# Forty-two elementwise instructions of a gated MLP layer moved from GpSimd to the Vector engine

## The chip, the cores and the metric

The kernel runs on one core of one Trainium2 chip. The metric is the time of one execution on the device in microseconds (us); of several runs the median counts. The engines are called as the profile calls them: PE (TensorE, with PEld for its weight loads), DVE (the Vector engine), ACT (the Scalar engine), POOL (GpSimd) and SP (the engine that issues most of the DMAs).

## What is computed

Three layers follow one another on B = 2 batches of S = 768 tokens.

```python
def _attn_ref(q, k, v, alpha):          # 8 heads of 48
    for t in range(S):
        state = alpha[:, :, t, :, None] * state + np.einsum('bhd,bhe->bhde', k[:, :, t], v[:, :, t])
        y[:, :, t] = np.einsum('bhd,bhde->bhe', q[:, :, t], state)
...
def _moe_ref(x, w_in, g_ln, w_sg, b_sg, w_out):   # d_model 384, d_ff 1024
    h = gelu(x @ w_in)
    u, v = h[..., :512], h[..., 512:]
    v_n = (v - mean(v)) / sqrt(var(v) + 1e-6) * g_ln
    v_s = np.einsum('ts,bsd->btd', w_sg, v_n) + b_sg[None, :, None]
    return x + (u * v_s) @ w_out
...
def _moe2_ref(x, w_gate, w_local, w1, w2):        # 8 experts
    # each token has one expert e: the argmax of its logits, or the expert of the token before it
    out[b, s] = p[e] * (np.maximum(x[b, s] @ w1[e], 0.0) @ w2[e])
```

The second layer is the one the change touches: x is the attention output, `u * v_s` is "the gate's product".

## The kernel before

**Split numbers.** Most products of the second and third layer are made from pairs. `split` (lines 160 to 162) takes a tile `src`: ACT writes its rounded high part (line 161), and an engine that the caller names writes the low part, `src` minus the high part (line 162). `mm3` (line 373) then issues three matmuls for each product: high by high, high by low, low by high.

**The engine is a table's choice.** `pick(way)` (line 157) returns DVE where the lowest bit of `way` is set, otherwise POOL. Three tables use it: `XS_E` for the low part of the attention output in `x_split` (12 pieces of 128x384: two batches, three row groups, two halves of the tokens); `NS_E` for the low part of the normalised v in `norm` (12 pieces of 128x512); and `SG` for the gate in `gmlp_s` (16 pieces), bit 0 for the product, bit 1 for the low part of that product.

**The gate, step by step** (`gmlp_s`, from line 478). For a batch b, a part hf of the tokens and one of four row groups d: PE adds up 18 matmuls in `pvs`; DVE scales it and adds the bias (line 493, tile `vs`); the engine of bit 0 multiplies by u (line 495); ACT writes the high part of the product into `g` (line 161) and the engine of bit 1 the low part (line 162). `gmlp_out` (line 499) multiplies the four `g` by `wo` on PE (`po`), DVE adds the result to x (line 511), and `route` (line 514) computes logits, keeps and expert slots: matmuls `pr` on PE, then a chain of short DVE instructions to `kf`, a matmul `pkr`, a DVE scan `er`, a matmul `pe`. Batch 0 has parts of 384 and 384 tokens, batch 1 of 512 and 256 (`SPL`).

```python
        eng = [self.pick(way), self.pick(way >> 1)]
...
        nc.vector.scalar_tensor_tensor(out=vs, in0=pv, scalar=self.gln[:, d:d + 1], in1=self.bsg[:, sl],
                                       op0=ALU.mult, op1=ALU.add)
        eng[0].tensor_tensor(out=vs, in0=vs, in1=us[d][:, sl], op=ALU.mult)
        self.split(hi, lo, vs, eng[1])
```

**What else runs beside the gate of batch 0.** The four pieces of `w_out` are prepared there (`w64_split`): on DVE four instructions each, in lines 318, 320, 321 and 324 (tile `w_wo`, 128x384), on ACT two, and on POOL the low part `wo_lo`. Then `x_split` of batch 1 (tile `xhl`).

**What sets the order.** A scheduler orders each engine's instructions ahead of time by its own estimate of when operands are there; an engine then runs its list strictly in that order, and an instruction whose operand is late holds up all behind it. A different engine for an instruction therefore also changes the order on other engines.

The stages in time of the profiled execution: attention with the first projections to about 145 us, then the gate and routing of batch 0, its counterpart of batch 1 from about 216 to 260, the experts from 274 to the end.

Of the kernel before, what the change touches and what calls it, by code (L numbers as in the profile page):

```python
# [60 lines left out]
XS = 16  # L61
SPL = (384, 512)
SELM = 0
SG = (0, 0, 2, 3, 0, 0, 0, 3, 2, 0, 0, 3, 0, 2, 0, 1)
XS_E = (0, 2, 0, 0, 0, 0, 1, 0, 0, 0, 0, 0)
NS_E = (0, 0, 0, 2, 1, 0, 2, 0, 0, 1, 3, 0)
XEE = 0
NUNIT = 21

# [3 lines left out]
class Layer:  # L73
# [329 lines left out]
    def x_split(self, b, xT):  # L403
        nc = self.nc
        xhl = []
        for k in range(KM):
            t = self.unit([P, 2, S], F32R, f"xhl_{b}_{k}")
            for hf in range(2):
                sl = slice(hf * HALF, (hf + 1) * HALF)
                self.split(t[:, 0, sl], t[:, 1, sl], xT[k][:, sl], self.pick(XS_E[b * 6 + k * 2 + hf]))  # L410
            xhl.append((t[:, 0], t[:, 1]))
        return xhl

    def gmlp_h(self, b, xhl, vhl, us, seq):
# [35 lines left out]
        def norm(j):  # L450
# [6 lines left out]
            for i in range(G):  # L457
                v2 = v2s[i]
                nc.scalar.activation(out=v2, in_=v2, func=AF.Identity, scale=vr[:, 1, i:i + 1], bias=vr[:, 0, i:i + 1])
                self.split(vh[:, i, :], vl[:, i, :], v2, self.pick(NS_E[b * 6 + len(vhl)]))  # L460
                vhl.append((vh[:, i, :], vl[:, i, :]))
# [16 lines left out]
    def gmlp_s(self, b, hf, d, vhl, us):  # L478
# [10 lines left out]
        hi, lo = self.gt[:, d % m, 0], self.gt[:, d % m, 1]  # L489
        way = SG[(2 * b + hf) * 4 + d]  # L490
        eng = [self.pick(way), self.pick(way >> 1)]
# [535 lines left out]
```

## Time and profile before

| | us |
|---|---|
| median of 3 runs (lowest, highest) | 429.46 (428.47, 433.92) |
| the profiled execution's own time | 431.54 |
| its span, first to last instruction | 429.8 |
| PE busy | 403.0 |
| DVE busy | 299.3 |
| POOL busy | 142.1 |
| mean granted TensorE clock | 0.889 of full speed |

[...] A row of the timeline gives start, duration, engine, line, operation, output and inputs, the shape, how many instructions were merged, and in brackets how long the engine had been idle before it and whom it waited for. A duration on DVE includes some 0.05 to 0.1 us in which the next instruction already runs, so rows of merged instructions are shorter than the sum.

### The profile page before, as it was taken

The page shows a single profiled execution, that of the slowest core. Times are in us where ns is not written, and L with a number is a line of the kernel's source. Part 1 is how long each engine was busy: PE and PEld are TensorE (multiplying, and loading weights), DVE is VectorE, ACT ScalarE, POOL GpSimd, SP SyncE. Part 2 cuts the span into 40 slices and gives each one's busy share as a digit, 9 for nine tenths or more (in the row PEclk, how much of TensorE's full clock was granted, in tenths as well). Part 3 has the DMA queues.
Part 4 walks back from the last instruction along what each step waited for, and adds up shares of the span by engine and source line. Part 5 has one row for each costly group of instructions (what it writes and reads, how often), then busy time and mean ns, then how long its engine had stood idle before and what let it go on. Part 6 is the DMA issues. An engine that isn't in the chain of part 4 may idle for free. (4 is left out here: it accounts for less than half of the span.)

```text
span 429.8 us, 7588 instructions
## 1 busy us (share of the span) xinstructions
PE 403.0 (94%) x2751; PEld 347.8 (81%) x2751; DVE 299.3 (70%) x694; ACT 202.1 (47%) x465; POOL 142.1 (33%) x156
## 2 busy tenths in 40 slices
PE   5899999999999996999999988999998999999992
PEld 2776666778886986798888885799888999999991
DVE  7969694954847698677866867673798866894220
ACT  2343443564787533426572432542793655763110
POOL 2315332754037457700304423375131110101101
PEclk9555555589999998999999998899998999999998
DMA  8993558220204220101060254958988457100000
GB/s 222 281 217 95 174 155 245 88 68 15 88 2 139 66 73 0 57 1 58 0 221 2 73 160 140 329 150 240 374 289 297 143 198 278 53 2 29 30 2 24
DMA packets 34742, 54.54 MB, mean 127 GB/s; under 512 B 6243, under 2 KB 24957, under 8 KB 34704
## 3 DMA queue, kind: packets, MB, share of 16 engines
q1 hardware_dynamic: 32528, 48.08, 35.7%
q0 software_dynamic: 2176, 5.98, 4.7%
q8 instruction: 22, 0.36, 0.4%
q14 instruction: 16, 0.13, 0.1%
HBM read 46.91 MB, written 5.55 MB: 122 GB/s over the span
## 5 line engine op out<-in xcount | busy, mean ns | idle before, releaser
L377 PE MATMUL pmy_e<-we_e_hi,hhl_e 128*128 128x384 f32 x256 | 68.5, 343 | 2.4 <-DVE hhl_e L756 1.8
L377 PE MATMUL ph_e<-xhl_e,we_e_hi 128*128 128x256 f32 x384 | 70.4, 284 | 0.1
L162 DVE TENSOR_TENSOR we_e_lo<-wr_e,we_e_hi 128x384 fp32r<-128x384 f32 (+1 forms) x112 | 61.5, 604 | 10.8 <-ACT we_e_hi L161 5.5
L161 ACT ACTIVATE we_e_hi<-wr_e 128x384 fp32r<-128x384 f32 (+1 forms) x112 | 54.6, 568 | 24.6 <-PE pmy_e L377 12.9
L377 PEld LDWEIGHTS ph_e<-xhl_e,we_e_hi 128*128 128x128 f32 x384 | 60.4, 191 | 0.6 <-DVE xhl_e L162 0.6
L770 POOL DMA_INDIRECT out_dram<-my_e,sid x16 | 20.5, 1280 | 105.8 <-DVE my_e L769 76.3
L377 PE MATMUL ph_e<-xhl_e,we_e_lo 128*128 128x256 f32 x192 | 54.1, 283 | 0.0
L377 PEld LDWEIGHTS pmy_e<-we_e_hi,hhl_e 128*128 128x128 f32 x256 | 47.2, 191 | 3.3 <-DVE hhl_e L756 2.0
L231 POOL TENSOR_SCALAR_AFFINE_SELECT at<-at 128x384 f32<-128x384 f32 x32 | 25.6, 820 | 64.9 <-ACT at L229 64.9
L377 PE MATMUL pmy_e<-we_e_lo,hhl_e 128*128 128x384 f32 x128 | 43.3, 339 | 0.1
L755 ACT ACTIVATE hhl_e<-ph_e 128x256 fp32r<-128x256 f32 x64 | 22.9, 385 | 40.9 <-PE ph_e L377 40.7
L377 PEld LDWEIGHTS ph_e<-xhl_e,we_e_lo 128*128 128x128 f32 x192 | 36.8, 192 | 0.0
L756 DVE SCALAR_TENSOR_TENSOR hhl_e<-ph_e,hhl_e 128x256 fp32r<-128x256 f32 x64 | 24.7, 416 | 15.0 <-ACT hhl_e L755 14.9
L377 PE MATMUL pvs<-sg_hi,v_hi 128*128 128x384 f32 (+2 forms) x96 | 32.9, 343 | 0.0
L377 PE MATMUL pvs<-sg_lo,v_hi 128*128 128x384 f32 (+2 forms) x96 | 32.1, 335 | 0.0
L377 PE MATMUL pvs<-sg_hi,v_lo 128*128 128x384 f32 (+2 forms) x96 | 31.1, 336 | 0.0
L279 PE MATMUL py<-at,io 128*64 128x128 f32 (+1 forms) x192 | 30.1, 383 | 0.0
L377 PE MATMUL po<-g,wo_hi 128*128 128x384 f32 (+2 forms) x96 | 26.3, 354 | 3.9 <-ACT g L161 3.2
L227 PE MATMUL sc<-io 48*128 48x128 f32 x192 | 29.1, 406 | 0.0
L262 ACT ACTIVATE state<-pds,bc 112x48 f32<-112x48 f32 x40 | 12.1, 301 | 34.8 <-PE pds L260 25.6
L227 PEld LDWEIGHTS sc<-io 48*128 48x128 f32 x192 | 22.5, 278 | 6.6 <-issue 3.7
L769 DVE TENSOR_SCALAR my_e<-pmy_e,xs_e 128x384 f32<-128x384 f32 x16 | 9.8, 611 | 21.9 <-PE pmy_e L377 21.7
(200 smaller groups left out, 876.0 us busy)
## 6 DMA issues: line engine op xcount, KB each, us to landing
wr_e<-in_moe_w_dram SPq DMA_DIRECT2D x32, 768.0 KB, 7.4
io<-in_alpha_dram SPq DMA_DIRECT2D x16, 169.8 KB, 5.0
io<-in_k_dram SPq DMA_DIRECT2D x16, 168.0 KB, 4.9
io<-in_q_dram SPq DMA_DIRECT2D x16, 168.0 KB, 5.0
io<-in_v_dram SPq DMA_DIRECT2D x16, 144.0 KB, 4.9
sraw<-in_moe_w_sg_dram SPq DMA_DIRECT2D x3, 768.0 KB, 4.5
x2d<-xt SPq DMA_DIRECT2D x12, 192.0 KB, 2.0
x<-y SPq DMA_DIRECT2D x24, 72.0 KB, 2.2
```

The source lines that it names most:

```text
L161: return (self.nc.scalar.activation(out=hi, in_=src, func=AF.Copy), eng.tensor_tensor(out=lo, in0=src, in1=hi.bitcast(F32), op=ALU.subtract))
L162: eng.tensor_tensor(out=lo, in0=src, in1=hi.bitcast(F32), op=ALU.subtract))
L227: nc.tensor.matmul(sc[j][:, cs], kf[r, cs], qf[r, cs], start=True, stop=True)
L231: nc.gpsimd.affine_select(out=at[:, j], in_=at[:, j], compare_op=ALU.is_ge, fill=0.0, base=0, pattern=[[0, NCH], [1, P]], channel_multipli ...
L262: nc.scalar.activation(out=state[:, s0 + c + 1, :], in_=pds[:112, cd], func=AF.Identity, scale=bc[:, c:c + 1])
L279: nc.tensor.matmul(py[64 * j:64 * j + m, cs], g["v"][:, o:o + m], at[:, j, c, :], start=True, stop=not inter)
L377: self.nc.tensor.matmul(out, l[a], r[c], start=start and i == 0 and p == 0, stop=stop and i == n - 1 and p == 2)
L755: nc.scalar.activation(out=hh, in_=ph, func=AF.Relu)
L756: nc.vector.scalar_tensor_tensor(out=hl, in0=ph, scalar=0.0, in1=hh.bitcast(F32), op0=ALU.max, op1=ALU.subtract)
L769: nc.vector.tensor_scalar(out=y, in0=py, scalar1=prob[i], scalar2=None, op0=ALU.mult)
L770: nc.gpsimd.indirect_dma_start(out=self.out2, out_offset=bass.IndirectOffsetOnAxis(ap=sid[:, i:i + 1], axis=0), in_=y, in_offset=None, bou ...
```

## The change

Three tables change, no other line. The gate's 16 products and 16 low parts, the 12 low parts of the attention output and the 12 of the normalised v all go to DVE. The pieces that leave POOL are 12 products, 10 low parts of the gate, 11 of the attention output and 9 of v: 42.

```diff
-SG = (0, 0, 2, 3, 0, 0, 0, 3, 2, 0, 0, 3, 0, 2, 0, 1)
-XS_E = (0, 2, 0, 0, 0, 0, 1, 0, 0, 0, 0, 0)
-NS_E = (0, 0, 0, 2, 1, 0, 2, 0, 0, 1, 3, 0)
+SG = (3,) * 16
+XS_E = (1,) * 12
+NS_E = (1,) * 12
```

On DVE, at about 77 to 90 us, where the attention's last two decays are prepared (`aw`, `io`) and the last pieces of `w_in` (`w_wu`), the low parts `xhl` of batch 0 now stand between them:

```order
 L200 COPY begins<-io_1_2_656 112x3
+L162 TENSOR_TENSOR xhl_0_790<-x_91,xhl_0_790 128x384
 L320 SCALAR_TENSOR_TENSOR w_wu_652<-w_wu_652 128x512
 L201 SCALAR_TENSOR_TENSOR aw_1_2_1027<-io_1_2_656,begins 112x384
+L162 TENSOR_TENSOR xhl_0_790<-x_91,xhl_0_790 128x384
+L162 TENSOR_TENSOR xhl_1_795<-x_92,xhl_1_795 128x384
 L321 SCALAR_TENSOR_TENSOR w_wu_652<-w_wu_652 128x512
+L162 TENSOR_TENSOR xhl_2_800<-x_93,xhl_2_800 128x384
 L202 COPY bc_1_2_1028<-aw_1_2_1027 112x3
 L207 TENSOR_TENSOR io_1_2_656<-io_1_2_656,aw_1_2_1027 112x384
```

The two remaining `xhl` pieces follow behind the next L203 and L204, ahead of the last decay.

On DVE in the gate of batch 0, first part, with the last piece of `w_out` (`w_wo_1563`); the scaling of pieces 2 and 3 (L493) now stands ahead of two of that weight's instructions, and both products and low parts follow:

```order
 L318 TENSOR_SCALAR w_wo_1563<-w_wo_1563 128x384
+L493 SCALAR_TENSOR_TENSOR vs_2_0_1645<-pvs_2_0_1625,gln,bsg 128x384
+L493 SCALAR_TENSOR_TENSOR vs_3_0_1669<-pvs_3_0_1650,gln,bsg 128x384
 L320 SCALAR_TENSOR_TENSOR w_wo_1563<-w_wo_1563 128x384
+L495 TENSOR_TENSOR vs_2_0_1645<-vs_2_0_1645,u_2_1275 128x384
+L495 TENSOR_TENSOR vs_3_0_1669<-vs_3_0_1669,u_2_1275 128x384
 L321 SCALAR_TENSOR_TENSOR w_wo_1563<-w_wo_1563 128x384
-L493 SCALAR_TENSOR_TENSOR vs_2_0_1645<-pvs_2_0_1625,gln,bsg 128x384
+L162 TENSOR_TENSOR g_0_2_1644<-vs_2_0_1645,g_0_2_1644 128x384
 L324 SCALAR_TENSOR_TENSOR w_wo_1563<-w_wo_1563 128x384
```

The low part of piece 3 closes that block, as it did before.

On DVE right behind it (`x_91` to `x_93` are the three row groups of batch 0's x, `xhl` the low parts of batch 1): the first addition of `po`, which PE's `pr` reads, now has three more instructions ahead of it.

```order
 L493 SCALAR_TENSOR_TENSOR vs_0_1_1709<-pvs_0_1_1689,gln,bsg 128x384
+L162 TENSOR_TENSOR xhl_0_1674<-x_94,xhl_0_1674 128x384
 L493 SCALAR_TENSOR_TENSOR vs_1_1_1733<-pvs_1_1_1714,gln,bsg 128x384
 L162 TENSOR_TENSOR xhl_0_1674<-x_94,xhl_0_1674 128x384
+L495 TENSOR_TENSOR vs_0_1_1709<-vs_0_1_1709,u_0_1036 128x384
+L495 TENSOR_TENSOR vs_1_1_1733<-vs_1_1_1733,u_0_1036 128x384
 L511 TENSOR_TENSOR x_91<-po_0_0_1763,x_91 128x384
+L162 TENSOR_TENSOR xhl_1_1679<-x_95,xhl_1_1679 128x384
 L511 TENSOR_TENSOR x_92<-po_1_0_1764,x_92 128x384
 L511 TENSOR_TENSOR x_93<-po_2_0_1765,x_93 128x384
+L162 TENSOR_TENSOR xhl_1_1679<-x_95,xhl_1_1679 128x384
+L162 TENSOR_TENSOR xhl_2_1684<-x_96,xhl_2_1684 128x384 x2
```

Behind them follow two low parts of `g`, two scalings, two products and, among the short instructions to `kf`, two more low parts of `g`.

## Rows read from the trace of the kernel before

**Rows 1.** The page: busy time and share of the span by engine.
```profile
PE 403.0 (94%) x2751; PEld 347.8 (81%) x2751; DVE 299.3 (70%) x694; ACT 202.1 (47%) x465; POOL 142.1 (33%) x156
```

**Rows 2.** Windows by stage: stretch, length, busy PE PEld DVE ACT POOL, clock, DMA.
```profile
145.00:160.00 15.00, 14.98 (x87) 14.66 (x86) 14.00 (x17) 6.26 (x14) 10.54 (x9) 1.00 0.24 77
160.00:164.00 4.00, 3.38 (x18) 2.81 (x17) 3.93 (x5) 1.22 (x3) 3.53 (x3) 1.00 0.00 0
164.00:167.00 3.00, 0.07 (x1) 0.00 (x0) 2.31 (x5) 1.22 (x3) 2.45 (x2) 0.95 0.00 0
167.00:170.00 3.00, 2.71 (x8) 2.71 (x9) 3.00 (x5) 1.89 (x5) 1.44 (x3) 0.50 0.00 0
170.00:183.00 13.00, 12.29 (x76) 10.79 (x75) 8.21 (x25) 4.67 (x11) 9.88 (x10) 1.00 0.15 48
205.00:212.00 7.00, 6.20 (x39) 5.31 (x38) 6.36 (x13) 2.84 (x7) 3.94 (x4) 1.00 0.00 0
```

**Rows 3.** Timeline of PE, 160 to 211 us.
```profile
161.19 0.45 PE L377 MATMUL po<-g,wo_hi 128*128 128x384 f32 x1 [0.61 <-POOL g L162]
...
167.29 1.65 PE L377 MATMUL po<-g,wo_hi 128*128 128x384 f32 x4 [3.23 <-ACT g L161]
...
171.81 0.86 PE L526 MATMUL pr<-rt,x 128*128 128x137 f32 x6
...
179.24 0.33 PE L563 MATMUL pkr<-identb,kf 128*1 128x128 bf16 x3
...
182.71 0.22 PE L587 MATMUL pe<-onesb,er 1*128 1x1 bf16 x3 [0.71 <-DVE er L570]
...
210.14 0.41 PE L617 MATMUL pe<-R,L 128*128 128x96 f16 x2 [0.37 <-DVE R L615]
```

**Rows 4.** Groups of POOL: busy us, mean ns of one, idle before.
```profile
L162 POOL TENSOR_TENSOR xhl<-x,xhl 128x384 fp32r<-128x384 f32 x11 | 13.1, 1218 | 0.0
L495 POOL TENSOR_TENSOR vs<-vs,u 128x384 f32<-128x384 f32 (+2 forms) x12 | 12.7, 1064 | 19.6 <-DVE vs L493 19.6
L162 POOL TENSOR_TENSOR v_lo<-v,v_hi 128x512 fp32r<-128x512 f32 x9 | 12.0, 1361 | 23.7 <-ACT v_hi L161 23.6
L162 POOL TENSOR_TENSOR g<-vs,g 128x384 fp32r<-128x384 f32 (+2 forms) x10 | 11.0, 1108 | 5.5 <-ACT g L161 5.5
```

**Rows 5.** Groups of DVE, one shape each.
```profile
L162 DVE TENSOR_TENSOR we_e_lo<-wr_e,we_e_hi 128x384 fp32r<-128x384 f32 x64 | 31.4, 546 | 5.1 <-ACT we_e_hi L161 5.0
L162 DVE TENSOR_TENSOR we_e_lo<-wr_e,we_e_hi 128x512 fp32r<-128x512 f32 x48 | 30.3, 682 | 5.8 <-PE pmy_e L377 2.6 <-issue 1.5 <-POOL vs L495 1.2
...
L204 DVE TENSOR_TENSOR_SCAN aw<-io,ends 112x384 f32<-112x384 f32 x16 | 16.8, 1052 | 0.1
...
L162 DVE TENSOR_TENSOR g<-vs,g 128x256 fp32r<-128x256 f32 x1 | 0.4, 416 | 0.0
```

**Rows 6.** Timeline of DVE, 153 to 210 us.
```profile
153.07 0.56 DVE L320 SCALAR_TENSOR_TENSOR w_wo<-w_wo 128x384 int32<-128x384 int32 x1
...
161.38 1.26 DVE L320 SCALAR_TENSOR_TENSOR w_wo<-w_wo 128x384 int32<-128x384 int32 x1
...
170.97 1.60 DVE L511 TENSOR_TENSOR x<-po,x 128x384 f32<-128x384 f32 x3 [0.92 <-PE po L377]
...
207.22 2.65 DVE L614 TENSOR_SCALAR L<-iota,cl 128x128 f16<-128x128 f16 x2
```

**Rows 7.** Timeline of POOL, 159 to 210 us.
```profile
159.81 2.43 POOL L162 TENSOR_TENSOR g<-vs,g 128x384 fp32r<-128x384 f32 x2 [0.64 <-ACT g L161]
162.19 1.34 POOL L162 TENSOR_TENSOR wo_lo<-w_wo,wo_hi 128x384 fp32r<-128x384 f32 x1
...
205.97 3.84 POOL L162 TENSOR_TENSOR v_lo<-v,v_hi 128x512 fp32r<-128x512 f32 x3
```

**Rows 8.** Timeline of ACT, then of DVE, 87 to 94 us.
```profile
87.59 0.52 ACT L161 ACTIVATE xhl<-x 128x384 fp32r<-128x384 f32 x1
...
93.35 0.69 DVE L385 SCALAR_TENSOR_TENSOR sq_v<-sq_v,pv 128x512 f32<-128x512 f32 x1 [4.46 <-ACT sq_v L384]
```

## The prediction

> **What bounds the kernel now.** I read first the page's busy times [rows 1]: PE is busy for 403.0 of 429.8 us, so the end moves only where PE gets a wait less or a wait more, or runs at another clock. POOL is busy for a third of the span, so its 42 instructions are worth nothing by their length alone. Then I looked in the windows for stretches where PE is not full [rows 2], and on PE's timeline for what ended the waits [rows 3].
>
> PE is full from 145 to 160. In the gate of batch 0 it has 0.62 us idle from 160 to 164 and 2.93 from 164 to 167, and then runs at clock 0.50, the lower level, for 3 us [rows 2]. The two waits there, 0.61 and 3.23 us, end with a low part from POOL and a high part from ACT [rows 3]. Further on PE waits 0.71 us for `er` [rows 3], and has 0.80 us idle between 205 and 212 [rows 2], where it waits for `R`, an input of the slot matmul [rows 3].
>
> The engine behind the long wait is DVE: 14.00 busy of 15 us, then 3.93 of 4, 2.31 of 3 and 3.00 of 3 [rows 2]. One cause shows in its rows: L320, on one shape, takes 0.56 us at 153.07 and 1.26 us at 161.38 [rows 6]. From 159.81 to 163.53 POOL works without a gap [rows 7]. The same stands at 207: two L614, whose operands are there, take 2.65 us and end at 209.87, when POOL's three `v_lo` end at 209.81 [rows 6, 7]. So a DVE instruction that meets a POOL instruction ends with it or a little later, and DVE loses about 0.7 us each time.
>
> **The change part by part.** *What moves.* POOL loses 42 instructions and 13.1 + 12.7 + 12.0 + 11.0 = 48.8 us [rows 4]. DVE gains them: by shape, from the tables, 22 of 128x384, 14 of 128x512 and 6 of 128x256, at 0.546, 0.682 and 0.416 us [rows 5] 12.0 + 9.5 + 2.5 = 24.0 us. Behind one another they need 0.5 us per 128x384 (three L511 take 1.60, [rows 6]). What counts is where the 24 us land.
>
> *Attention's low parts of batch 0 (77 to 95 us): nothing, at most 1.3 us lost.* DVE's list now holds `xhl` pieces among the last decays. The second half of `xhl_1` needs ACT's high part, which starts at 87.59 and ends at 88.1 [rows 8]; DVE waits for it with three scans of 1.05 [rows 5] behind it, three products of about 0.65, two `xhl` of 0.55 and short ones, together about 6.4 us, an estimate. So DVE reaches `sq_v` at some 94.6 instead of 93.35 [rows 8], and the v chain starts 1.3 us late. DVE had been idle for 4.46 us there, which is the cover. PE wants nothing of that chain before the bank that v's first tile frees, and it has other matmuls to do; I take 0.
>
> *Low parts of v, batch 0: 0.* PE is full through them [rows 2]; PE first has v's other row tiles to read.
>
> *Gate of batch 0, first part.* From 145 to 160 DVE receives two `v_lo`, two products and two low parts, 2 x 0.68 + 4 x 0.5 = 3.4 us, and loses meetings with POOL at 0.7 each; I count five, an estimate, 3.5 us. So I let it reach the L318 of the last weight near 160.0, against 160.17. From there by the new order: L318 0.4, two scalings 1.1, L320 meeting the third `wo_lo`, 0.7, two products 1.0, L321 0.6, a low part 0.5, L324 0.4, a low part 0.5: 165.2. Before, POOL's and DVE's queue had PE wait until 167.29. PE ends its 18 matmuls for pieces 0 and 1 at 163.1 and can go on at 164.2; its remaining 15 take 2.7 us at full clock, to 166.9. Before, it came to `pr` at 171.81 [rows 3]: 4.9 us won at that point.
>
> *What is late next.* Most of it is given back at once. Ahead of `x_91`, which `pr` reads, DVE now has two scalings 1.1, an `xhl` that meets the last `wo_lo` 1.0, a second `xhl` 0.5, two products 1.0 and the addition 0.5: 165.2 + 4.1 = 169.3. PE stands idle for 2.4 us, and the gain is 171.81 - 169.3 = 2.5. Behind that DVE has, by the new order, two additions, four `xhl` and two low parts, 8 x 0.48 = 3.9 (to 173.2); two scalings and two products, 2.1 (to 175.3); three reductions, two low parts and the short chain, 2.2, of which the first `kf` needs all but 0.3: 177.1 (the last two figures estimates, from 0.5 for a long instruction and 0.15 to 0.2 for a short one). PE has by then done its 18 `pvs` and nine `pv` matmuls (5.9 us, to 175.7), so it waits 1.4 us and issues `pkr` at 177.15 against 179.24 [rows 3]. The scan `er` follows in 2.2 us, to 179.4, while PE has nine more `pv` of 0.23, to 179.9; the 0.71 us wait is gone. `pe` is at 179.9 against 182.71: **2.8 us won**. Bounds: 4.9 if `x_91` isn't late; 0 if DVE loses the 2.4 us that stand between (half a dozen instructions at 0.5).
>
> *Clock.* PE's 2.4 us of waiting may bring the clock down as the 2.93 us did, after which 3 us ran at 0.50 [rows 2]. That is 1.5 us of work lost; part of it falls into the 1.4 us wait before `pkr`. Bounds 0 and 1.5; the idle time is near the one that did it, so I take **1.0 lost**.
>
> *Low parts of v, batch 1 (205 to 212 us).* POOL's three `v_lo` go, so L614 and L615 run at their own pace; three `v_lo` of 0.6 stand behind them, and DVE ends about a microsecond sooner. PE's 0.80 us goes: **0.8 won**.
>
> *Gate of batch 1: 0.* DVE gets 6 x 0.68 and 6 x 0.42, about 6.5 us, in a stretch where PE has no wait of note and DVE gaps; the last part (from 252) has the tight chain into routing, where a low part of 0.4 us is added and a meeting with POOL of about 0.5 goes. Bounds -0.5 and +0.5.
>
> *Experts: 0.* No instruction of theirs changes engine; they follow the routing, and so do the loads.
>
> Sum: -2.8 + 1.0 - 0.8 = -2.6 us. The profiled execution's own 431.54 becomes 428.9. That execution stands 2.08 us over the median of the runs, so from 429.46 I predict **426.9 us**. A change that a measurement of this kernel can tell from none is about 2%, some 8.6 us; this is not one.
>
> **Rivals.** *No gain.* DVE bounds the whole of 145 to 183: any slip of 2 to 3 us there leaves `kf` where it was, and only the 0.8 us stays, or nothing: 428.5 to 430.5. For it: DVE's 6.6 idle us in those 38 [rows 2] shrink by 18 instructions, 2 x 0.68 + 16 x 0.5 = 9.4 us. Against it: the meetings with POOL.
>
> *Full gain.* `x_91` isn't late and the clock stays: 4.9 + 0.8, perhaps 0.5 more from the routing: 423 to 425. For it: six more meetings between 160 and 172 that I price at 0.7 only. Against it: the seven instructions counted before the addition.
>
> *Slower.* DVE's long instructions aren't POOL's doing, or `wo_lo` and `sg_lo`, which stay on POOL, go on causing them. Then all 9.4 us stay and only 6.6 idle us take them up; the place is `kf` of batch 0, first part, whose `pkr` comes 2.8 us after 179.24, and with a second clock fall (1.5) and the 0.8 won the time is 429.46 + 2.8 + 1.5 - 0.8 = 433.0. It decides if L320 and L321 of the last two weights still take 1.26 us each. [...]
>
> **How the numbers follow.** Forecast with its bounds (425.0 to 428.5): 0.55. No gain (428.5 to 430.5): 0.18. Full gain (422 to 425): 0.14. Slower (430.5 to 435): 0.13. The range for 8 in 10 leaves a little of both ends out: 422.5 to 431.5. Faster by over 2% needs under 420.9, which only a full gain with something unseen on top reaches: 0.04. Slower by over 2% needs over 438: 0.03. Within 2%: 0.93.
>
> **What would show it.** In the profile of the changed kernel: L320 near 0.56 us except beside `wo_lo`; PE's wait before `po` of piece 2 under 1 us instead of 3.23; a new wait of about 2.4 us at the first `pr` of batch 0, ended by L511 on DVE, and about 1.4 us at `pkr` ended by `kf`; no wait for `R` near 208; and at 92 to 145 no wait on PE. Wrong would be: waits on PE between 92 and 145; `pr` without a wait; `pkr` later than 179.24; or a change in the experts' own length, 274 us to the end.

## The result and the profile after

The changed kernel's median is 410.82 us in 4 runs (407.48 to 425.49). The kernel before, run beside it, has 429.33 us in 4 runs (428.47 to 433.92). The ratio is 0.952, with a 95% interval of 0.942 to 0.963: faster, and below the predicted range of 422.5 to 431.5. This ratio, and every ratio below, compares only those runs of each kernel that lie within 1.5% of its own fastest run (here the one of 425.49 us is left out), while medians count all runs; the experiments show that the runs left out stand at levels that both kernels have.

The profiled execution took 411.53 us, with a span of 409.8. On the page, first the busy times of the changed kernel, then its clock in 40 equal slices of the span:

```profile
PE 384.9 (94%) x2751; PEld 337.2 (82%) x2751; DVE 306.8 (75%) x736; ACT 202.0 (49%) x465; POOL 94.5 (23%) x114
PEclk9599855999999998999999998996999999999998
```

and the clock of the kernel before:

```profile
PEclk9555555589999998999999998899998999999998
```

POOL has lost its 42 instructions and 47.6 us against [rows 1]. DVE has gained 42 instructions and only 7.5 us. But PE, which got no instruction more or less, is busy for 18.1 us less. The same matmuls in less time point to a higher clock, and the two clock rows say where: in slices 2 to 8 of the kernel before every digit is 5. In the changed kernel slices 3 to 5 read 9, 9 and 8.

The windows of the attention show it. Columns as in [rows 2]. First the changed kernel, then the kernel before:

```profile
10.00:20.00 10.00, 8.05 (x68) 6.51 (x70) 9.51 (x22) 3.20 (x8) 4.20 (x6) 0.50 1.04 290
20.00:47.00 27.00, 26.05 (x310) 18.14 (x308) 26.97 (x50) 15.23 (x41) 12.65 (x12) 1.00 0.86 231
47.00:72.00 25.00, 25.00 (x201) 18.11 (x201) 24.09 (x46) 12.71 (x32) 12.07 (x11) 0.52 0.64 183
72.00:88.00 16.00, 16.00 (x135) 12.51 (x136) 13.37 (x23) 9.43 (x23) 5.72 (x6) 1.00 0.22 54
```

```profile
20.00:47.00 27.00, 27.00 (x197) 19.00 (x194) 20.17 (x40) 10.81 (x28) 7.65 (x7) 0.50 0.64 170
47.00:72.00 25.00, 25.00 (x181) 16.61 (x179) 19.74 (x36) 9.86 (x24) 9.51 (x10) 0.50 0.67 196
72.00:88.00 16.00, 16.00 (x134) 11.86 (x131) 14.71 (x23) 8.23 (x21) 10.14 (x9) 0.50 0.35 99
```

From 20 to 47 us PE does 310 matmuls at clock 1.00 in the one and 197 at 0.50 in the other; these two readings are the clock's upper and lower level in what follows. By the first `pv`, the first matmul behind the attention's longest part (72.9 us against 89.6), the changed kernel leads by 16.7 us. Its first moved instruction, a low part of `xhl` on DVE, starts at 65.35 us. Up to there each engine does the same instructions in both programs, and at 20 us, where the clock parts, nothing that the change touches has run yet.

What the change does in its own stretch stands in PE's timeline of the changed kernel:

```profile
146.51 1.23 PE L377 MATMUL po<-g,wo_hi 128*128 128x384 f32 x4
...
152.23 0.97 PE L526 MATMUL pr<-rt,x 128*128 128x137 f32 x6 [2.03 <-DVE x L511]
...
154.41 0.52 PE L377 MATMUL pvs<-sg_hi,v_lo 128*128 128x384 f32 x1
...
161.28 0.33 PE L563 MATMUL pkr<-identb,kf 128*1 128x128 bf16 x3
...
191.16 0.30 PE L617 MATMUL pe<-R,L 128*128 128x96 f16 x3
```

The wait of 3.23 us in [rows 3] is gone: `po` of piece 2 follows without an entry in brackets. In its place PE waits 2.03 us for the addition of L511 at the first `pr`. Behind that the matmuls take 0.52 us instead of 0.33, until 156.65 us: the lower clock. At `R` (191.16) there is no wait. On DVE and POOL:

```profile
135.66 0.56 DVE L320 SCALAR_TENSOR_TENSOR w_wo<-w_wo 128x384 int32<-128x384 int32 x1
136.25 1.26 DVE L321 SCALAR_TENSOR_TENSOR w_wo<-w_wo 128x384 int32<-128x384 int32 x1
...
146.23 0.54 DVE L321 SCALAR_TENSOR_TENSOR w_wo<-w_wo 128x384 int32<-128x384 int32 x1
...
187.70 0.42 DVE L614 TENSOR_SCALAR L<-iota,cl 128x128 f16<-128x128 f16 x2
```

```profile
135.99 1.10 POOL L162 TENSOR_TENSOR wo_lo<-w_wo,wo_hi 128x384 fp32r<-128x384 f32 x1 [2.70 <-ACT wo_hi L161]
```

L320, which starts ahead of a `wo_lo` on POOL, takes 0.56 us; L321 right behind it meets that `wo_lo`, ends 0.4 us after it and takes 1.26. The L321 of the last weight meets none and takes 0.54. The two L614 take 0.42 us against 2.65 in [rows 6].

So there are two questions: how much is the change's own, and does the clock in the attention have to do with it? For the first I count from the first `pv`. The starts of the first `pv`, the first `pvs` and the first `px` (the experts' gather) are from the views of these tiles; the differences are worked out from them. Two columns matter: `pvs` to `px` holds the gate and routing of both batches, that is nearly all of what the change touches.

| kernel (profiled execution) | first `pv` | first `pvs` | first `px` | span | `pvs` to `px` | `px` to end |
|---|---|---|---|---|---|---|
| before | 89.6 | 135.7 | 265.4 | 429.8 | 129.7 | 164.4 |
| after | 72.9 | 119.4 | 245.5 | 409.8 | 126.2 | 164.3 |

From the first `pv` to the end it is 340.2 us before and 336.9 after. Of the 20.0 us between the two spans 16.7 lie ahead of the first `pv`, and 3.3 behind it. The first `pv` isn't a clean cut for every pair, though: where the lower clock reaches past it, the stretch from there to the first `pvs` is longer (46.1 to 49.5 us in the profiles of this document, 49.4 in one kernel whose program there is that of the kernel before). `pvs` to `px` is the safer column.

### The profile page after: what moved, and what is told of

It is laid out like the page before. It is cut to its first block, busy times and chain, and to the rows that moved or that the text cites. A ratio compares the mean times of both kernels' runs of the same rounds, so it can differ in the third digit from the quotient of the medians.

```text
span 409.8 us, 7572 instructions
## 1 busy us (share of the span) xinstructions
PE 384.9 (94%) x2751; PEld 337.2 (82%) x2751; DVE 306.8 (75%) x736; ACT 202.0 (49%) x465; POOL 94.5 (23%) x114
## 5 line engine op out<-in xcount | busy, mean ns | idle before, releaser
L377 PE MATMUL ph_e<-xhl_e,we_e_hi 128*128 128x256 f32 x384 | 73.1, 290 | 1.5 <-issue 1.3
L377 PE MATMUL pmy_e<-we_e_hi,hhl_e 128*128 128x384 f32 x256 | 67.0, 337 | 1.0 <-issue 1.0
L377 PEld LDWEIGHTS ph_e<-xhl_e,we_e_hi 128*128 128x128 f32 x384 | 62.6, 198 | 1.7 <-issue 1.1
L377 PEld LDWEIGHTS ph_e<-xhl_e,we_e_lo 128*128 128x128 f32 x192 | 38.1, 199 | 1.6 <-issue 1.6
L231 POOL TENSOR_SCALAR_AFFINE_SELECT at<-at 128x384 f32<-128x384 f32 x32 | 28.1, 899 | 48.4 <-ACT at L229 48.4
L279 PE MATMUL py<-at,io 128*64 128x128 f32 (+1 forms) x192 | 25.2, 334 | 0.0
L377 PE MATMUL po<-g,wo_hi 128*128 128x384 f32 (+2 forms) x96 | 24.8, 342 | 0.0
L377 PE MATMUL pv<-wv_hi,xhl 128*128 128x512 f32 x72 | 24.7, 402 | 0.0
L377 PEld LDWEIGHTS pmy_e<-we_e_lo,hhl_e 128*128 128x128 f32 x128 | 24.1, 188 | 0.7 <-issue 0.7
L377 PE MATMUL pu<-xhl,wu_hi 128*128 128x384 f32 x96 | 24.5, 343 | 0.0
```

The source lines that it names most:

```text
L231: nc.gpsimd.affine_select(out=at[:, j], in_=at[:, j], compare_op=ALU.is_ge, fill=0.0, base=0, pattern=[[0, NCH], [1, P]], channel_multipli ...
L279: nc.tensor.matmul(py[64 * j:64 * j + m, cs], g["v"][:, o:o + m], at[:, j, c, :], start=True, stop=not inter)
L377: self.nc.tensor.matmul(out, l[a], r[c], start=start and i == 0 and p == 0, stop=stop and i == n - 1 and p == 2)
```

## The experiments

Theory A: the 16.7 us come from the clock's level in the attention, which differs from run to run of either kernel; the change's own share is the 3.3. Theory B: something of the moved instructions sets the level.

### One instruction, and one table at a time

```diff
-SG = (0, 0, 2, 3, 0, 0, 0, 3, 2, 0, 0, 3, 0, 2, 0, 1)
+SG = (0, 0, 2, 3, 0, 0, 0, 3, 2, 0, 0, 3, 0, 2, 0, 3)
```

> Of the whole change only one instruction is made: the low part of the last gate piece of batch 1 (128x256, at some 255 us of the kernel before) goes to DVE. Up to 250 us the program is that of the kernel before. In the changed kernel PE's first pv came 16.7 us earlier (72.86 against 89.58 us), although both programs are the same up to 77 us; TensorE's clock had risen at 20 us there and only at 87 us before. Theory A (the clock's level in the attention is a matter of small time differences that any program may meet, not of the moved instructions): some runs here may show it too, with a mean clock of 0.93 or more and about 411 to 414 us, others 0.89 and 429. Theory B (something of the moved instructions or of their place sets the level): every run is at 428 to 431 us with a clock of 0.88 to 0.90, first pv at 89 to 90 us.

```diff
-XS_E = (0, 2, 0, 0, 0, 0, 1, 0, 0, 0, 0, 0)
+XS_E = (1,) * 12
```

> Only the low parts of the attention output go to DVE (11 instructions). They begin at some 77 us. If they carry the early gain (theory B, by what stands first in the program), the time is about 412 and the first pv at 73 us, clock 0.93 or more. By theory A the runs lie at 412 or at 429, without a link to the table. At an equal clock in the attention I expect 0 to -0.5 us from this table.

```diff
-NS_E = (0, 0, 0, 2, 1, 0, 2, 0, 0, 1, 3, 0)
+NS_E = (1,) * 12
```

> Only the low parts of the normalised v go to DVE (9 instructions, from 110 us on). At an equal clock in the attention -0.8 us, from the wait for R near 208 us that goes: 428.6. Theory A: some runs may be at 411 to 413 with a clock of 0.93 or more; theory B, if it isn't this table: all near 428.6.

```diff
-SG = (0, 0, 2, 3, 0, 0, 0, 3, 2, 0, 0, 3, 0, 2, 0, 1)
+SG = (3,) * 16
```

> Only the gate's products and low parts go to DVE (22 instructions, from 150 us on). At an equal clock in the attention -1 to -3 us: the wait before po of piece 2 of batch 0 (3.23 us) shrinks, pe of batch 0 comes 1.5 to 2.8 us earlier behind the first pv: 427 to 428. Theory A: some runs may be 16 us below that with a clock of 0.93 or more; theory B, if it isn't this table: none.

Measured, 6 runs each, with 11 runs of the kernel before on the same chip:

| kernel | lowest | median | highest | ratio to before, 95% interval |
|---|---|---|---|---|
| before | 410.98 | 425.86 | 431.17 | |
| one instruction | 410.73 | 419.19 | 432.05 | 0.996 (0.985 to 1.006) |
| XS_E alone | 410.57 | 423.14 | 429.18 | 0.995 (0.976 to 1.014) |
| NS_E alone | 411.43 | 420.85 | 426.21 | 1.004 (0.985 to 1.022) |
| SG alone | 407.33 | 412.19 | 431.77 | 0.989 (0.977 to 1.001) |

The kernel before, untouched, has runs of 411 and of 431 us here. So does the one with a single instruction changed, which starts at 239.58 us there. Theory B as it was stated falls for the 16.7 us: the gain that it was to explain turns up in the kernel without the change. A weaker form of it, that the change makes the upper level more frequent, is not tested by this and comes up again below. The mean clock in the records mostly goes with the times: 0.95 and 0.96 in the two runs of before under 415 us, 0.885 to 0.904 in the six over 425. Five of the runs over 425 us in this document, of several kernels, have 0.977 to 0.990; the last section says why that reading is not to be trusted.

In the window table the parts show all the same, since it leaves the attention out:

| kernel | first `pv` | first `pvs` | first `px` | span | `pvs` to `px` | `px` to end |
|---|---|---|---|---|---|---|
| one instruction | 68.4 | 117.8 | 247.3 | 409.1 | 129.5 | 161.7 |
| XS_E alone | 86.9 | 133.4 | 263.9 | 425.2 | 130.5 | 161.2 |
| NS_E alone | 77.5 | 124.7 | 251.6 | 413.5 | 126.9 | 161.9 |
| SG alone | 68.5 | 117.9 | 244.9 | 406.4 | 126.9 | 161.5 |

Against 129.6 (the mean of before and of one instruction) SG alone wins 2.7 us, NS_E alone 2.7, and XS_E alone loses 0.9. The sum, 4.5, is about 1 above the 3.4 of all three together. My expectation for NS_E was 0.8 and for XS_E 0 to 0.5 won: both were off. With NS_E alone the wait of 0.61 us at `po` is gone as well as the one at `R`. XS_E's loss may be the clock's: the waits at `po` are 0.60 and 3.20 us, as before, but PE runs at the lower level for 5.8 us behind the second of them instead of 2.8. One profile each doesn't tell a difference of 1 us from that: two profiles of the whole change differ by 1.5 us in this stretch (below).

### Filling PE's early waits

If the 3.30 us wait at 8.6 us is where the attention loses the clock, matmuls on constant data in it should settle the level. The first two kernels have

```diff
-                nc.tensor.matmul(sc[j][:, cs], kf[r, cs], qf[r, cs], start=True, stop=True)
+                last = nc.tensor.matmul(sc[j][:, cs], kf[r, cs], qf[r, cs], start=True, stop=True)
+        if u == "0_0_0":
+            self.fill(14, last)
```

> The kernel before with 14 matmuls on constant data (128x512, result unused) behind the first twelve sc, where PE waits 3.30 us (8.6 to 11.9). They take 0.22 us each at the upper level: 3.1 us, in time that PE had idle. Theory A, in the form that this wait is where the attention loses the clock: matmuls stay at the upper level behind 12 us, py at 0.27 to 0.31 us instead of 0.42, first pv near 68, most runs at 408 to 413 us. Rival C (the attention's own narrow matmuls don't keep the clock up whatever stands ahead of them): runs spread over 409 to 432 as those of the kernel before do.

> The same fill in the changed kernel. If the fill settles the clock in both kernels, the two compare at one level and the change itself shows: 2.6 to 3.5 us below the filled kernel before. If the 16.7 us were the change's own, it would be 16 us or more below. Rival C: both spread, and the fastest runs of either differ by 3 us.

and the other two, besides,

```diff
-WARM0 = 10
+WARM0 = 14
```

> As the filled kernel before, with 14 instead of 10 matmuls at the start as well, which cover the other early wait (1.30 us, 5.9 to 7.25). If the first wait alone brings the clock down in some runs (a trace has pkt at the lower level at 7.83 us), this is steadier than the fill of the second wait alone: all runs within 1%, 408 to 412 us. If the fill settles nothing, it spreads like the rest.

> The changed kernel with both early waits filled: 404 to 408 us in nearly all runs if the clock is settled by them, 2.6 to 3.5 us under the same fill in the kernel before. Else 405 to 430.

| kernel | runs | lowest | median | highest | ratio to before, 95% interval |
|---|---|---|---|---|---|
| before | 29 | 408.49 | 419.27 | 431.75 | |
| before, second wait filled | 12 | 414.93 | 424.29 | 430.93 | 1.011 (0.994 to 1.029) |
| after, second wait filled | 12 | 416.51 | 417.83 | 426.59 | 1.015 (1.010 to 1.021) |
| before, both filled | 6 | 411.81 | 424.51 | 429.60 | none on record |
| after, both filled | 12 | 412.36 | 422.86 | 427.83 | 1.010 (0.999 to 1.021) |

The fill doesn't settle the clock: three of the four kernels spread, as Rival C of the expectations had it. Its other half failed: the fastest runs of the two kernels with the second wait filled differ by 1.6 us, with the changed kernel the slower one, where 3 us the other way were expected. The changed kernel with the second wait filled is steady (11 of 12 runs within 3.1 us), at a level that is neither the high nor the low one. Why it is steady and its counterpart of the kernel before, with the same instructions up to 71 us, is not, stays open. The steady kernel's trace shows where the upper level ends in spite of the fill. PE, then the windows:

```profile
32.90 0.45 PE L262 MATMUL pds<-state,ident 64*64 64x48 f32 x4 [1.97 <-ACT state L264]
```

```profile
20.00:30.00 10.00, 10.00 (x129) 7.25 (x128) 9.94 (x22) 4.99 (x14) 4.13 (x4) 1.00 0.87 246
30.00:35.00 5.00, 3.03 (x24) 1.87 (x26) 5.00 (x10) 2.68 (x8) 2.26 (x2) 0.79 0.51 124
35.00:40.00 5.00, 5.00 (x39) 3.73 (x35) 5.00 (x12) 2.50 (x7) 2.17 (x2) 0.50 0.78 224
```

With the fill PE is at the upper level by 20 us (129 matmuls from 20 to 30 us). But at that level the attention is no longer bound by PE: DVE is busy for 9.94 of 10 and 5.00 of 5 us, PE for 3.03 of the same 5, it waits 1.97 us for a `state` from ACT, and the clock falls (0.79, then 0.50). At the lower level PE is full again (5.00 of 5 us), and it stays there until the clock rises, at about 81 us.

The pairs give the change's own share at matched clocks:

| kernel | first `pv` | first `pvs` | first `px` | span | `pvs` to `px` | `px` to end |
|---|---|---|---|---|---|---|
| before, second wait filled | 80.6 | 127.5 | 256.6 | 419.0 | 129.1 | 162.4 |
| after, second wait filled | 82.1 | 129.0 | 254.9 | 417.0 | 125.9 | 162.1 |
| before, both filled | 85.7 | 132.6 | 261.9 | 421.9 | 129.3 | 160.0 |
| after, both filled | 88.9 | 135.7 | 261.5 | 421.8 | 125.8 | 160.3 |

That is 3.2 and 3.5 us won from `pvs` to `px`, and 3.5 in the first pair of all. From the first `pv` to the end the three pairs give 3.3, 3.5 and 3.3 us.

### The change once more, a better choice, and less DVE work in the attention

The first kernel is the changed one without an edit.

> The changed kernel once more, for its spread beside the kernel before on the same chip. Theory A (the 16.7 us come from the clock's level in the attention, which differs from run to run of either kernel): the runs spread from 407 to 430 us, some of them at 0.89 to 0.91 of the full clock and 424 to 429 us, and the median lies 2 to 8 us from that of the kernel before. Theory B (the change itself brings the level up): nearly all runs at 407 to 412 us while the kernel before spreads.

The second leaves the low parts of the attention output on POOL as before:

```diff
-SG = (0, 0, 2, 3, 0, 0, 0, 3, 2, 0, 0, 3, 0, 2, 0, 1)
-NS_E = (0, 0, 0, 2, 1, 0, 2, 0, 0, 1, 3, 0)
+SG = (3,) * 16
+NS_E = (1,) * 12
```

> The gate's and v's parts on DVE, the low parts of the attention output back on POOL as before. From the first pvs to the first px the kernels so far took 129.1 to 129.7 us (kernel before, with and without fill, and with one instruction changed), 126.1 and 125.8 (all three tables), 127.0 (SG alone), 126.9 (NS alone), 130.5 (XS_E alone). If the parts add up, this takes 129.5 - 2.5 - 2.6 = 124.4 us, 1.5 less than the whole change; rival: SG and NS save the same wait and it takes 126. The time itself spreads with the clock.

The third and fourth take 32 short copies off DVE, from the kernel before and from the second:

```diff
-        V.tensor_copy(out=self.begins[:, 0::P], in_=al[:, HALF + 1:])
+        self.nc.scalar.activation(out=self.begins[:, 0::P], in_=al[:, HALF + 1:], func=AF.Copy)
...
-        V.tensor_copy(out=bc, in_=dq[:, P - 1::P])
-        V.reciprocal(out=self.ends[:, P - 1::P], in_=bc)
+        self.nc.scalar.activation(out=bc, in_=dq[:, P - 1::P], func=AF.Copy)
+        V.reciprocal(out=self.ends[:, P - 1::P], in_=dq[:, P - 1::P])
```

> The kernel before with 32 short copies of the attention (lines 200 and 202) on ACT instead of DVE, some 11 us of DVE between 3 and 88 us; ACT has 40 us of them idle. In the runs that start at the upper level DVE is busy all the time from 20 to 60 us, PE waits for it, and the level falls. If those waits are what takes the clock down, PE waits less here, the first pv comes at 62 to 68 us in most runs and the times lie at 402 to 412. Rival: the fall has nothing to do with DVE (or ACT's queue becomes the wait): times spread over 408 to 432 as before.

> Both edits: gate and v parts on DVE, the short copies on ACT. If both do what they are for: 398 to 408 us in most runs, 4 to 5 us under the relieved kernel before. If the copies don't settle the clock: 404 to 428.

Measured, 6 runs each and 11 of the kernel before, with the stretches of the profiled executions:

| kernel | lowest | median | highest | ratio to before, 95% interval | first `pv` | `pvs` to `px` | `px` to end |
|---|---|---|---|---|---|---|---|
| before | 408.61 | 429.33 | 431.81 | | | | |
| after again | 407.65 | 414.10 | 426.73 | 0.999 (0.975 to 1.023) | 90.5 | 124.7 | 161.0 |
| SG and NS_E | 403.95 | 412.55 | 422.82 | 0.983 (0.953 to 1.013) | 89.4 | 124.1 | 161.4 |
| before, copies on ACT | 413.63 | 423.83 | 432.95 | 1.010 (0.990 to 1.030) | 89.2 | 129.5 | 161.6 |
| SG, NS_E, copies on ACT | 414.26 | 421.67 | 429.89 | 1.011 (0.991 to 1.031) | 74.7 | 126.8 | 161.6 |

The changed kernel spreads as theory A has it, from 407.65 to 426.73. In its profiled execution of 426.73 us the first `pv` starts at 90.5 us, later than in the kernel before. The ratio reads 0.999 here; in the first series, with 0.952, no run of the kernel before lay under 428 us. Over all series the kernel before has 55 runs from 408.49 to 433.92 and the changed one 10 from 407.48 to 426.73; their lowest runs differ by 1.0 us, their highest by 7.2.

One figure doesn't fit theory A as I had stated it. The medians here lie 15.2 us apart (414.10 against 429.33), where it expected 2 to 8. Of the changed kernel's 10 runs 8 are under 416 us, of the 55 of the kernel before 14; with the change's own 3.3 us allowed for (before under 419.3) it is 22. So the changed kernel may well meet the upper level more often. No experiment here separates that from chance: ten runs in two series are few, and the runs of a series need not be independent. What is shown is that the kernel before reaches the same levels, not that both reach them equally often.

SG and NS_E without XS_E take 124.1 us from `pvs` to `px`, where adding the parts had given 124.4. PE's timeline of this kernel:

```profile
166.50 0.79 PE L377 MATMUL po<-g,wo_lo 128*128 128x384 f32 x3 [0.70 <-POOL wo_lo L162]
167.85 0.97 PE L526 MATMUL pr<-rt,x 128*128 128x137 f32 x6 [0.56 <-DVE x L511]
```

Without the `xhl` pieces ahead of it the addition is late by 0.56 us instead of 2.03, and the clock stays up behind it. But the fourth kernel has the same three tables and takes 126.8 us. There, PE, DVE and POOL:

```profile
157.81 1.59 PE L526 MATMUL pr<-rt,x 128*128 128x137 f32 x6 [2.64 <-DVE x L511]
154.66 2.62 DVE L495 TENSOR_TENSOR vs<-vs,u 128x384 f32<-128x384 f32 x2
154.27 6.12 POOL L162 TENSOR_TENSOR xhl<-x,xhl 128x384 fp32r<-128x384 f32 x5
```

The two products ahead of the addition take 2.62 us beside POOL's five `xhl` (1.01 in the changed kernel, at 150.70), the addition is late by 2.64 us, and the clock falls: the six `pr` take 1.59 us, against 0.97 in the second kernel. So it depends on where POOL's `xhl` fall whether leaving them there is worth anything; that XS_E costs something is not shown.

For the second kernel: from the first `pv` to the end this execution takes 421.0 - 89.4 = 331.6 us. The kernel before, with its first `pv` at 89.6, takes 340.2, of which 3.0 are the experts' (164.4 against 161.4). From `pvs` to `px` it beats both kernels, before by 5.5 us (129.6 to 124.1) and the whole change by 0.5 to 2.0 (124.7 to 126.2). At 0.983 (0.953 to 1.013) its time alone doesn't show that, since the attention's clock hides it.

The copies on ACT didn't settle the clock. In the fourth kernel PE waits 1.77 us for a `state` from ACT at 59.50 us, and the clock falls there; in the third PE stays at the lower level from 12 to 90 us without such a wait. Most falls come with a wait on PE: in seven of the nine profiles that show a fall in the attention behind 12 us, a wait of 1.3 to 2.7 us stands at it or up to 2 us ahead of it (1.31 us in the kernel before with the second wait filled, 2.73 in the one with a single instruction changed). In the other two, the changed kernel among them, the longest wait there is 0.4 us. In the changed kernel it comes some 2 us ahead of the fall at 47.5:

```profile
45.35 0.48 PE L227 MATMUL sc<-io 48*128 48x128 f32 x2 [0.42 <-ACT at L229]
```

What ended the level there stays open, and so does what lets it begin at 20 us in one run and at 88 in the next. Both executions' PE timelines from 17 us on look alike to 0.06 us, until the clock parts them. After, then before:

```profile
19.46 0.69 PE L279 MATMUL py<-at,io 128*64 128x128 f32 x4
19.92 0.52 PE L250 MATMUL pds<-io,kt 128*48 128x48 f32 x8
20.36 0.51 PE L219 MATMUL pkt<-ident,io 112*128 112x112 f32 x3
20.80 0.93 PE L227 MATMUL sc<-io 48*128 48x128 f32 x10
```

```profile
19.40 0.69 PE L279 MATMUL py<-at,io 128*64 128x128 f32 x4
19.86 0.63 PE L250 MATMUL pds<-io,kt 128*48 128x48 f32 x8
20.42 0.82 PE L219 MATMUL pkt<-ident,io 112*128 112x112 f32 x3
21.17 1.65 PE L227 MATMUL sc<-io 48*128 48x128 f32 x10
```

## Why the prediction was wrong, and where it was right

By its own steps, first `pv` as the common start, after against before:

**Low parts of the attention output, 0, at most 1.3 lost.** The first `pvs` came 46.5 us behind the first `pv`, against 46.1, without a wait on PE in either; in the filled pairs 46.9 each time. Right for these pairs, within 0 to 1.3. The stretch also takes 48 to 49.5 us in profiles where the lower clock reaches into it, with and without the change. What XS_E puts ahead of the addition was counted there.

**First part of the gate of batch 0.** The order's reading held. The 3.23 us wait went; the addition of `x_91` became late, and PE waited 2.03 us for L511 where 2.4 was forecast. The first `pr` came 2.9 us earlier (79.4 behind the first `pv`, against 82.2), forecast 2.5. That DVE's long instructions are meetings with POOL held too: 0.54 us for L321 without one, 1.26 for L321 with one, and the two L614, 2.65 us beside POOL's `v_lo` in [rows 6, 7], take 0.42 without it. The prediction had every such meeting cost DVE some 0.7 us; not every one does: in the kernel before, the L493 at 155.84 us takes 0.60 us inside two products of POOL (155.53, 2.35 us), and the L493 at 137.43 of the changed kernel takes 0.60 with POOL idle. What decides it is not shown by any run here. The rival "slower", by which those lengths weren't POOL's doing, is out.

**`pkr` and `pe`.** `pkr` came 1.3 us earlier instead of 2.1, and without the 1.4 us wait of the forecast. The clock had fallen right behind the wait at `pr`, so PE was slow while DVE caught up:

```profile
150.00:153.00 3.00, 0.97 (x9) 0.77 (x7) 3.00 (x7) 2.11 (x5) 0.00 (x0) 1.00 0.01 3
153.00:157.00 4.00, 4.00 (x16) 4.00 (x15) 3.45 (x8) 0.00 (x0) 0.00 (x0) 0.57 0.00 0
```

The clock is 0.57 over four microseconds. `pe` came 1.7 us earlier; the forecast was 2.8 less 1.0 for the clock, 1.8. The clock term was of the right kind. The second profile of the changed kernel shows its size: there PE waits 2.02 us at the same place, the matmuls behind it take 0.33 us, and `pvs` to `px` is 124.7 instead of 126.2, 1.5 us where 1.0 was forecast. Without the fall `pe` would have come some 3.2 us earlier (1.7 + 1.5), not 2.8. So it is in part luck that 1.7 lies so near 1.8: the gain and the clock's price were each larger than forecast by half a microsecond.

**Low parts of v, batch 1, 0.8 won.** It was 1.5: 1.5 us more are won between `pe` and the last `pu` (last `pu` 123.0 us behind the first `pv`, against 126.2). The term was mis-sized. I had added up PE's idle time in the window, 0.80 us in [rows 2]. The starts tell more: the last `pu` ahead of the three `pe` starts at 209.43 us before, the next `pu` at 211.18, 1.75 us; after, 190.98 and 191.29, 0.31 us. The idle times don't hold all that such a gap costs. NS_E alone shows the same: from `pe` to the last `pu` 31.6 us, against 33.1 with one instruction changed and 33.1 before.

**Gate of batch 1 and experts, 0.** Last `pu` to first `px`: 49.6 us in both (265.4 - 215.8 and 245.5 - 195.9). (The prediction gives DVE six instructions of 128x512 there; by the tables it is five, with no effect on the term.) Experts: 164.4 and 164.3. Right, the second by luck: both of these executions took 2 to 4 us more there than the others (160.0 to 162.4), with other waits in each.

**The sum.** The forecast for the change's own share was 2.6 us; it was 3.3, 3.5 and 3.3 in three pairs.

**The step that failed** is the last one of the sum: "The profiled execution's own 431.54 becomes 428.9. That execution stands 2.08 us over the median of the runs, so from 429.46 I predict 426.9 us." That step takes all that the change doesn't touch to last as long in every run, on the word of three runs from 428 to 434. The attention doesn't: its 78 us from 10 to 88 stood at clock 0.50 in the profile, and the same instructions, for the most part at the other level, take up to 21 us less (first `pv` at 68.4 instead of 89.6; some 3 of these are gone again by the first `pvs`, 117.8 against 135.7). The three runs shown lay at 428 to 434 us, three of the four runs after at 407 to 412; less the change's own 3.3 us, that is some 15 of the 18.5 us between the medians. Whether three of four runs met the upper level by luck, or because the change makes that likelier, stays open. No rival held this. I had read the clock for PE's waits in the gate and never for the longest stretch at the lower level. The chance of 0.04 for faster by over 2% and the range were therefore too tight: 14 of the 55 runs of the unchanged kernel are below 415.5 us.

## What to carry to other kernels

When a stretch of a profile stands at the lower clock although PE is full (here 27.00 of 27 us busy at 0.50), treat its level as a variable: ask what the stage would take at the other one, and widen the range by that. Before a gain is put down to a change, look whether it lies ahead of the first instruction that moved, and compare stretches of traces behind that point, not whole times. When work moves off a neighbour whose instructions lengthen this engine's, count the meetings that go as well: DVE's 42 new instructions, 24.0 us by their lengths, made it busy for 7.5 us more. And count what the new order puts ahead of the next instruction that PE waits for: here the 3.23 us wait at `po` went, and 2.03 us came back at `pr`.

## What the runs showed of the hardware

The recorded clock can contradict the lengths of the matmuls for a long stretch. In the second profile of the changed kernel (426.73 us, mean clock 0.99):

```profile
20.00:47.00 27.00, 27.00 (x196) 19.00 (x193) 20.10 (x38) 10.87 (x28) 7.51 (x7) 1.00 0.61 163
```

```profile
21.09 1.65 PE L227 MATMUL sc<-io 48*128 48x128 f32 x10
```

The clock reads 1.00, but ten `sc` take 1.65 us as they do at 0.50, not 0.93, and 196 matmuls fit into the 27 us, not 310. The length of one kind of matmul is the better witness here: the first `pv` comes at 90.5 us, against 89.6 in the kernel before at 0.50. The profile of XS_E alone (mean clock 0.98) reads the same way: 1.00 from 20 to 47 us, and 196 matmuls.

The lower clock doesn't always follow the same wait: 2.03 us at `pr` was followed by matmuls of 0.52 us in one run of the changed kernel, 2.02 us by matmuls of 0.33 in another.

A stage can have another limit at each level of the clock: at the lower one PE is full in the attention (27.00 of 27 us, DVE 20.17), at the upper one DVE is (26.97 of 27, PE 26.05). In seven of the nine profiles that show the upper level end in the attention, it did so at a wait of PE of 1.3 to 2.7 us or up to 2 us behind one.
